# A gated linear attention with a mixture of attention experts on one core: the table that sets the order of the work is drawn anew

## The chip, the cores and the metric

The kernel runs on one core of one Trainium2 chip. The metric is the device time of one execution in microseconds (us). Each of the core's engines takes its own instructions in order and waits on semaphores for the others: PE (TensorE, matrix products and transposes), DVE (VectorE), ACT (ScalarE), POOL (GpSimd) and SP (SyncE, which here only issues DMA transfers). All of this kernel's transfers, loads and stores, are issued from SP.

## The reference, cut to what matters

```
for t in range(768):                                  # 4 batches x 8 heads, D = 48
    state = alpha[t] * state + outer(k[t], v[t])
    y[t] = q[t] @ state
x = heads of y side by side                           # 4 x 768 x 384
top two of four experts per token, by x @ w_gate; w = their softmax
for e in range(4):                                    # causal attention of one head of 64
    a = softmax(mask(x @ wq[e] @ (x @ wk[e]).T / 8))
    out += (w of e, 0 if not chosen) * (a @ (x @ wv[e]) @ wo[e])
```

## The kernel before

**Tiles.** The time axis is cut into 24 chunks of 128 steps, chunk n = 6 * batch + c. Each chunk has three inputs: `al` (the decays, 258.5 KB), `qk` (512 KB) and `vt` (v, 256 KB). Each of the three has four buffers (al_71 to al_74, qk_75 to qk_78, vt_79 to vt_82), so a load waits until the chunk that held its buffer is done with it. A chunk goes through: scan of the decays backwards (DVE L470) with its reciprocal (L474); scan forwards (L493); k times the backward products (L497) and q times the forward products (L501), the two instructions that need `qk`; the 128 x 128 products of q and k (PE L537), masked on DVE (L548) or on ACT and POOL (L552, L556); transposes of k (PE L570, copied on ACT); the state's update (PE L589, DVE L601 or L604, POOL L606, ACT L611), which needs `vt`; the chunk's output (PE L635), which needs `vt` too, and its split into a rounded part xh (ACT L651) and a rest xl (DVE L655). A check of the decays (ACT L513) reads `al` last and sets its buffer free. For the first three chunks the output goes to the buffer x32 instead (ACT L660).

Three chunks make one unit of the expert part, of which there are eight: projections to q and k (PE L683, or the fp32 form at L910 for unit 0, copied out at L691 to L695) and to v and the gate (L702, L710), scores (L772), their row maximum (DVE L782), exponentials (ACT L791), scaling by the chosen expert's weight (DVE L803, L804, POOL L810), transposes (PE L828, copied at L842), the product with v (L865) and with wo (L891), and the store (SP L899). Unit 0 also splits the weights in two parts (DVE L412 to L423).

**The order.** `build` lists all 1574 operations once, each with what it reads and writes. `schedule` walks the table `ORDER`, a permutation of their numbers, and works out a start for each from its own costs of operations and DMAs; from these starts come two things only: which buffer of a kind each tile gets, and how many idle matmuls (`warm`, L1118) stand at the very start of PE's queue where the model has PE wait. `emit` then issues the operations in the order of the table. Each engine works through its part of that list in order, so the table alone decides what stands behind what on PE, DVE, ACT and POOL, and in which order SP issues the transfers: a load that waits for its buffer holds every later load and store on SP.

**Loads.** load_al (L381), load_q (L385), load_v (L390), the weights wqk (L395), wvg and wo (L397, L398). In the trace the n-th transfer is issued only when the (n - 8)-th has landed. The table asks for chunk 5's three inputs twice.

Of the kernel before, what the change touches and what calls it, by code (L numbers as in the profile page):

```python
# [17 lines left out]
B, H, S, D = 4, 8, 768, 48  # L18
# [31 lines left out]
DMA_FIXED = 1.5  # L50
DMA_RATE = 400.0
# [92 lines left out]
def turnover(a, b):  # L144
    a, b = FORM[a], FORM[b]
    return 0.0 if a == b else NEAR.get(a + b, LEAVE[a] + ENTER[b])


class Plan:

# [1079 lines left out]
```

## Time and profile before

| | us |
|---|---|
| three runs | 317.69, 317.56, 316.7; median 317.56 |
| the profiled execution's own time | 316.78 |
| its span in the trace | 315.0 |
| PE busy | 302.0, 96% of the span |
| PE weight loads | 269.6, 86% |
| DVE busy | 246.6, 78% |
| ACT busy | 225.5, 72% |
| POOL busy | 118.7, 38% |

The granted TensorE clock is 1.00 through the whole span. PE is busy nearly everywhere, so what is left besides PE's own work is the stretch at the start in which the first data arrive, some short waits of PE, and the tail behind its last product. The page of the profile says how long each engine was busy; which wait cost something is read from the chain of waits and from each engine's timeline, where a bracket gives the idle time ahead of a group of instructions and what ended it.

### The profile page before, as it was taken

What the parts mean: (1) busy time and instruction counts of PE and PEld (TensorE: products, weight loads), DVE (VectorE), ACT (ScalarE), POOL (GpSimd) and SP (SyncE); (2) the same over time, 40 slices, a digit from 0 to 9 for tenths busy, and PEclk for the clock granted to TensorE, in tenths of its full rate; (3) what the DMA queues carried; (4) which work ended last, traced back from release to release, by engine and by line L of the source; (5) the groups of instructions that cost most, each with busy time, mean ns of one, the idle gap of its engine ahead of it and who ended that gap; (6) DMA issues with size and microseconds to landing.
All of it is one profiled execution on the core that took longest, in us unless ns stands there. A gap on an engine that the chain in (4) does not pass through costs nothing.

```text
span 315.0 us, 9747 instructions
## 1 busy us (share of the span) xinstructions
PE 302.0 (96%) x3786; PEld 269.6 (86%) x3786; DVE 246.6 (78%) x711; ACT 225.5 (72%) x592; POOL 118.7 (38%) x188
## 2 busy tenths in 40 slices
PE   6798999999999999999999999989999999999994
PEld 4697989999899799989988977979989978797883
DVE  6899999998999999997897998559677565658440
ACT  2476777689877796779488894468778797479681
POOL 4053144435256326216425341162454315316240
PEclk9999999999999999999999999999999999999999
DMA  6967363161340236415611530412100010010111
GB/s 208 406 233 238 126 233 140 34 201 62 127 145 25 73 145 207 139 31 195 222 38 36 189 108 0 152 56 74 37 17 2 27 51 2 1 52 25 52 52 57
DMA packets 15027, 33.25 MB, mean 106 GB/s; under 512 B 1664, under 2 KB 4992, under 8 KB 14976
## 3 DMA queue, kind: packets, MB, share of 16 engines
q1 hardware_dynamic: 14976, 32.58, 30.3%
q8 instruction: 31, 0.51, 0.6%
q14 instruction: 20, 0.16, 0.2%
HBM read 27.86 MB, written 4.72 MB: 103 GB/s over the span
## 4 chain that ended last, share of the span: by engine, by line
PE 75%; DVE 10%; DMA 9%; issue 1%; SPq 1%; POOL 1%; ACT 1%; DVEq 0%; POOLq 0%
PE g L683 12%; PE g L828 11%; PE g L865 11%; PE g L772 10%; PE g L635 9%; DMA qk<-in_qk_dram 9%; PE g L891 8%; PE g L537 5%; PE g L710 5%; PE g L589 2%; PE g L570 2%; DVE al L493 2%; DVE a L782 1%; POOL a L810 1%; DVE qk L497 1%
## 5 line engine op out<-in xcount | busy, mean ns | idle before, releaser
L810 POOL TENSOR_SCALAR a<-a,cf,gw 128x256 f32<-128x256 f32 (+5 forms) x96 | 81.9, 863 | 90.4 <-DVE cf L804 60.4
L791 ACT ACTIVATE a<-a,mx 128x128 f32<-128x128 f32 (+5 forms) x96 | 63.4, 663 | 16.5 <-DVE mx L782 16.1
L842 ACT ACTIVATE at<-g 128x512 f32<-128x512 f32 (+3 forms) x124 | 50.3, 462 | 9.5 <-PE g L828 8.8
L782 DVE CUSTOM_DVE_ANT_0 a<-g,cm 128x512 f32<-128x512 f32 (+3 forms) x96 | 48.1, 529 | 8.6 <-PE g L772 7.0
L828 PE MATMUL g<-ident,a 128*128 128x128 f32 x336 | 45.4, 276 | 1.5 <-POOL a L810 0.7
L828 PEld LDWEIGHTS g<-ident,a 128*128 128x128 f32 x336 | 37.6, 141 | 5.9 <-POOL a L810 2.2
L865 PE MATMUL g<-at,vg 128*64 128x384 f32 (+2 forms) x324 | 39.5, 390 | 0.0
L772 PE MATMUL g<-k,q 64*128 64x256 f32 (+3 forms) x384 | 38.4, 334 | 0.0
L865 PEld LDWEIGHTS g<-at,vg 128*64 128x64 f32 x324 | 24.1, 137 | 13.6 <-issue 8.6
L635 PE MATMUL g<-ms,vt 128*32 128x128 f32 x768 | 32.8, 274 | 0.4 <-DVE mx L782 0.4
L772 PEld LDWEIGHTS g<-k,q 64*128 64x128 f32 x384 | 29.9, 185 | 3.7 <-DVE mx L782 0.8
L470 DVE TENSOR_TENSOR_SCAN al<-al,d1r 112x516 f32<-112x516 f32 (+1 forms) x25 | 29.9, 1200 | 3.8 <-DMA al<-in_al_dram 3.8
L556 POOL TENSOR_SCALAR_AFFINE_SELECT ms<-ms 128x512 f32<-128x512 f32 x23 | 14.6, 637 | 47.1 <-ACT ms L552 47.0
L493 DVE TENSOR_TENSOR_SCAN al<-al,d1c 112x516 f32<-112x516 f32 (+1 forms) x25 | 31.7, 1268 | 0.1
L683 PE MATMUL g<-xh,wqk_h 128*128 128x384 f32 x84 | 29.1, 346 | 0.0
L683 PE MATMUL g<-xh,wqk_l 128*128 128x384 f32 x84 | 28.3, 337 | 0.0
L683 PE MATMUL g<-xl,wqk_h 128*128 128x384 f32 x84 | 28.3, 336 | 0.0
L513 ACT ACTIVATE al<-al 112x1033 f32<-112x1033 f32 x24 | 25.5, 1064 | 2.7 <-POOL a L810 1.5
L537 PE MATMUL g<-qk 48*128 48x128 f32 x384 | 25.1, 276 | 0.0
L537 PEld LDWEIGHTS g<-qk 48*128 48x128 f32 x384 | 23.4, 187 | 1.2 <-issue 0.3
L635 PE MATMUL g<-qk,S 112*32 112x128 f32 x480 | 24.2, 272 | 0.0
L606 POOL TENSOR_TENSOR C<-C,ev 112x192 f32<-112x192 f32 x16 | 12.9, 808 | 29.0 <-DVE C L604 21.4
(103 smaller groups left out, 636.4 us busy)
## 6 DMA issues: line engine op xcount, KB each, us to landing
qk<-in_qk_dram SPq DMA_DIRECT2D x24, 512.0 KB, 4.7
vt<-in_v_dram SPq DMA_DIRECT2D x25, 256.0 KB, 3.5
al<-in_al_dram SPq DMA_DIRECT2D x24, 258.5 KB, 2.9
out_dram<-ot SPq DMA_DIRECT2D x24, 192.0 KB, 1.9
at<-in_wqk_dram SPq DMA_DIRECT2D x1, 768.0 KB, 7.9
qk<-in_qk_dram SPq DMA_DIRECT2D x2, 256.0 KB, 4.2
at<-in_wvg_dram SPq DMA_DIRECT2D x1, 390.0 KB, 9.5
at<-in_wo_dram SPq DMA_DIRECT2D x1, 384.0 KB, 9.8
```

The source lines that it names most:

```text
L470: V.tensor_tensor_scan(backwards(al[0:P, AW + c0 - 1:AW + c1 - 1]), backwards(al[0:P, c0:c1]), d1r[0:P, sl].rearrange("p a w -> p (a w)"), ...
L493: V.tensor_tensor_scan(c, c, T(("d1c", n))[0:P, sl].rearrange("p a w -> p (a w)"), 0.0, OP.mult, OP.max)
L537: PE.matmul(T(("pa", n, s))[:, C * p:C * p + C], t[r:r + D, p, C:2 * C], t[r:r + D, p, 0:C], start=True, stop=True, tile_position=(r, 0))
L635: PE.matmul(py[32 * j:32 * j + 32, k], l, r, start=(i == 0), stop=(i == len(parts) - 1), tile_position=(0, 32 * j))
L683: PE.matmul(pj[:, :W3], w[:, kt, cs], x[:, kt, :], start=(i == 0), stop=(i == 8))
L772: PE.matmul(T(sk[e])[:, :w], q[r, x, ts], k[r, y, c0:c1], start=(m == 0), stop=(m == 2), tile_position=(64 * e, 0))
L782: V.tensor_tensor_reduce(T(ak[e])[:, c0:c1], T(sk[e])[:, :w], cm[:, m0:m0 + w], -1.0, mx[:, 0:1] if x else BIG, OP.add, OP.min, accum_out= ...
L791: A.activation(a[:, 0:n], a[:, 0:n], AF.Exp, bias=T(mk)[:, e, len(pieces) - 1:len(pieces)], scale=-1.0, accum_out=T(("sm", u))[:, ix:ix + 1])
L810: G.tensor_scalar(a[:, 0:n], a[:, 0:n], T(ck_)[:, e:e + 1], T(("gw", u))[:, i, eg:eg + 1], op0=OP.mult, op1=OP.mult)
L828: PE.transpose(pt[:, 128 * (j - j0):128 * (j - j0) + 128], a[:, 128 * j:128 * j + 128], ident)
L842: A.activation(dst, src, AF.Copy)
L865: PE.matmul(py[64 * e:64 * e + 64, lo:n1], v[:, j % 3, 64 * eg:64 * eg + 64], at[e][:, at_off(j) + lo:at_off(j) + n1], start=(j == 0), sto ...
```

## The change

The table is another permutation of the same 1574 operations: the same instructions on each engine, in another order. The constants of the model's DMA become slower: 1.7 us and 390 KB/us instead of 1.5 us and 400 KB/us, and 240 KB/us until 8 us after the start (`DMA_EARLY`, in the new function `landing`); the separate rate of the weights is dropped. The table was drawn with these costs, and judged on runs of the model in which DMAs are late by a random amount. The number of idle matmuls at the start goes from 33 (23, 5 and 5) to 43 (32 and 11). Lines of the new kernel stand 1 to 7 further down: L381, L385 and L390 are L388, L392 and L397 there, L497 and L501 are L504 and L508, L655 is L662.

```diff
-DMA_FIXED = 1.5
-DMA_RATE = 400.0
+DMA_FIXED = 1.7
+DMA_RATE = 390.0
+DMA_EARLY = (8.0, 240.0)
...
 ORDER = (
-    13, 4, 14, 6, 0, 2, 7, 8, 1, 3, 10, 21, 31, 22, 60, 23, 9, 32, 24, 26, 25, 34, 28, 33, 15, 30, 35, 61, 16, 27, 36,
...
+    4, 6, 0, 7, 2, 21, 31, 22, 32, 14, 8, 13, 1, 3, 10, 9, 18, 23, 17, 60, 33, 24, 26, 34, 36, 25, 61, 57, 35, 68, 27,
...
+def landing(t, kb, rate):
+    until, early = DMA_EARLY
+    first = min(kb, max(0.0, until - t) * early)
+    return t + first / early + (kb - first) / rate
...
-                dma_at = max(t + DMA_FIXED, dma_at) + o["dma"] / (o["rate"] or DMA_RATE) / 1e3
+                dma_at = landing(max(t + DMA_FIXED, dma_at), o["dma"] / 1e3, o["rate"] or DMA_RATE)
...
-                op("S", 0.43, 0, lambda T: SY.dma_start(wqk(T), wqk_d), w=whole(("at", -2)), dma=786432, rate=360)
+                op("S", 0.43, 0, lambda T: SY.dma_start(wqk(T), wqk_d), w=whole(("at", -2)), dma=786432)
...
-                op("S", 0.43, 0, lambda T: SY.dma_start(wv(T), wv_d), w=[(("at", -1), 0)], dma=399360, rate=360)
-                op("S", 0.43, 0, lambda T: SY.dma_start(wo(T), wo_d), w=[(("at", -1), 1)], dma=393216, rate=360)
+                op("S", 0.43, 0, lambda T: SY.dma_start(wv(T), wv_d), w=[(("at", -1), 0)], dma=399360)
+                op("S", 0.43, 0, lambda T: SY.dma_start(wo(T), wo_d), w=[(("at", -1), 1)], dma=393216)
```

**SP at the start**, behind the loads of chunks 0 and 1 up to qk_76. Before, vt_80 is chunk 1, al_73 and qk_77 are chunk 3, vt_81 is chunk 8, al_74 and qk_78 are chunk 2, and chunk 2's v is two rows below the last one shown:

```order
L390 DMA vt_79<-in_v_dram 128x512
L390 DMA vt_80<-in_v_dram 128x512
L381 DMA al_73<-in_al_dram 128x517
L385 DMA qk_77<-in_qk_dram 128x1024
L395 DMA at_136<-in_wqk_dram 128x1536
L390 DMA vt_81<-in_v_dram 128x512
L381 DMA al_74<-in_al_dram 128x517
L385 DMA qk_78<-in_qk_dram 128x1024
L397 DMA at_138<-in_wvg_dram 128x780
L398 DMA at_138<-in_wo_dram 128x768
L381 DMA al_72<-in_al_dram 128x517
L390 DMA vt_82<-in_v_dram 128x512
```

Now, al_73 and qk_77 are chunk 2, al_74 and qk_78 chunk 3, vt_80 is chunk 1, vt_81 chunk 4 and vt_82 chunk 2:

```order
L397 DMA vt_79<-in_v_dram 128x512
L402 DMA at_136<-in_wqk_dram 128x1536
L388 DMA al_73<-in_al_dram 128x517
L388 DMA al_74<-in_al_dram 128x517
L397 DMA vt_80<-in_v_dram 128x512
L392 DMA qk_77<-in_qk_dram 128x1024
L397 DMA vt_81<-in_v_dram 128x512
L392 DMA qk_78<-in_qk_dram 128x1024
L404 DMA at_138<-in_wvg_dram 128x780
L405 DMA at_138<-in_wo_dram 128x768
L397 DMA vt_82<-in_v_dram 128x512
L388 DMA al_72<-in_al_dram 128x517
```

Chunk 2's qk moves from the fourteenth to the twelfth load and chunk 3's takes the fourteenth place; chunk 2's v moves from the twentieth place to the seventeenth.

**DVE at the start**, from the update of the state of chunk 1. Before, chunk 2 is al_74 with qk_78 and chunk 3 is al_73 with qk_77:

```order
L604 TENSOR_TENSOR C_93<-g_69,C_92 112x192
L474 RECIPROCAL d1c_87<-al_74 112x4
L497 TENSOR_TENSOR qk_78<-qk_78,al_74 112x4x128
L493 SCALAR_TENSOR_TENSOR al_74<-al_74,d1c_87 112x516
L695 TENSOR_TENSOR k_103<-g_67,k_103 128x128
L501 TENSOR_TENSOR qk_78<-qk_78,al_74 112x4x128
```

Now chunk 2 is al_73 with qk_77, and chunk 3 al_74 with qk_78:

```order
L611 TENSOR_TENSOR C_93<-g_63,C_92 112x192
L504 TENSOR_TENSOR qk_77<-qk_77,al_73 112x4x128
L481 RECIPROCAL d1c_87<-al_73 112x4
L504 TENSOR_TENSOR qk_78<-qk_78,al_74 112x4x128
L500 SCALAR_TENSOR_TENSOR al_73<-al_73,d1c_87 112x516
L702 TENSOR_TENSOR k_104<-g_67,k_104 128x128
L508 TENSOR_TENSOR qk_77<-qk_77,al_73 112x4x128
```

The k product of chunk 3 moves up to behind that of chunk 2, ahead of chunk 2's forward scan.

**SP some 198 us into the execution.** Before, vt_82 is chunk 23, qk_75 is chunk 20 and qk_76 chunk 21:

```order
L899 DMA out_dram<-ot_144 128x384
L385 DMA qk_76<-in_qk_dram 128x1024
L381 DMA al_74<-in_al_dram 128x517
L390 DMA vt_82<-in_v_dram 128x512
L385 DMA qk_75<-in_qk_dram 128x1024
L899 DMA out_dram<-ot_145 128x384
```

Now chunk 20 is qk_76 (and chunk 23's qk is qk_77), and chunk 23's v, vt_80 in the last row, stands behind three more loads:

```order
L392 DMA qk_77<-in_qk_dram 128x1024
L392 DMA qk_76<-in_qk_dram 128x1024
L906 DMA out_dram<-ot_145 128x384
L397 DMA vt_79<-in_v_dram 128x512
L388 DMA al_74<-in_al_dram 128x517
L392 DMA qk_78<-in_qk_dram 128x1024
L906 DMA out_dram<-ot_145 128x384
L397 DMA vt_80<-in_v_dram 128x512
```

The load of chunk 20's qk no longer stands behind the load of a v that is wanted three chunks later.

**DVE at the same place**, where the rests xl of two chunks of unit 6 are formed (xl_99). Before, qk_75 is chunk 20:

```order
L497 TENSOR_TENSOR qk_76<-qk_76,al_71 112x4x128
L782 ISA a_135,mx_116<-g_63,cm 128x384
L782 ISA mx_116 128x1
L655 TENSOR_TENSOR xl_99<-g_66,xh_97 128x3x128
L501 TENSOR_TENSOR qk_75<-qk_75,al_73 112x4x128
L782 ISA a_129,mx_119<-g_68,cm 128x128
L782 ISA mx_119 128x1
L655 TENSOR_TENSOR xl_99<-g_69,xh_97 128x3x128
L803 TENSOR_SCALAR cf_122<-sm_114 128x2
```

Now qk_76 is chunk 20:

```order
L662 TENSOR_TENSOR xl_99<-g_68,xh_97 128x3x128
L789 ISA a_128,mx_120<-g_67,cm 128x128
L789 ISA mx_120 128x1
L662 TENSOR_TENSOR xl_99<-g_69,xh_97 128x3x128
L508 TENSOR_TENSOR qk_77<-qk_77,al_71 112x4x128
L810 TENSOR_SCALAR cf_123<-sm_114 128x2
L811 RECIPROCAL cf_123<-cf_123 128x2
L504 TENSOR_TENSOR qk_76<-qk_76,al_72 112x4x128
```

Both rests stand ahead of the first instruction that needs chunk 20's qk; before, one stands behind it.

**At 149 us**, SP's queue held, before, the qk of chunks 19 and 17, the v of 18, the qk of 16, the v of 19, and then the qk of 18. Now it holds the v of 16 and the qk of 16, 18 and 19, then a store, and only then the v of 18 and 19, the decays of 23 and the v of 17. Further up, chunk 5's second load of v (vt_79) now stands behind the decays and the qk of chunk 6 and the v of chunk 6; before, it stood ahead of the first two.

## Rows read from the trace of the kernel before

**Rows 1.** The page: span, and engines by busy time, share and instructions.

```profile
span 315.0 us, 9747 instructions
...
PE 302.0 (96%) x3786; PEld 269.6 (86%) x3786; DVE 246.6 (78%) x711; ACT 225.5 (72%) x592; POOL 118.7 (38%) x188
```

**Rows 2.** Windows: stretch, length, busy time of PE, PEld, DVE, ACT, POOL, clock, DMA share, GB/s.

```profile
0.00:20.00 20.00, 15.14 (x205) 12.31 (x209) 14.97 (x29) 8.12 (x16) 6.89 (x37) 1.00 0.76 278
20.00:40.00 20.00, 19.15 (x299) 17.54 (x288) 19.52 (x50) 14.08 (x40) 4.55 (x8) 1.00 0.61 200
200.00:220.00 20.00, 18.40 (x221) 17.33 (x220) 11.94 (x39) 13.55 (x44) 6.83 (x11) 1.00 0.29 98
```

**Rows 3.** The chain of waits: start, length, what. A DMA runs from issue to landing.

```profile
8.78 9.23 DMA qk<-in_qk_dram
...
150.57 6.65 DMA qk<-in_qk_dram
...
198.08 5.80 DMA qk<-in_qk_dram
```

**Rows 4.** DVE timeline, start: start, length, instruction, count, idle before and what ended it.

```profile
15.28 1.23 DVE L470 TENSOR_TENSOR_SCAN al<-al,d1r 112x516 f32<-112x516 f32 x1 [1.31 <-DMA al<-in_al_dram]
...
18.03 0.69 DVE L497 TENSOR_TENSOR qk<-qk,al 112x512 f32<-112x512 f32 x1 [0.58 <-DMA qk<-in_qk_dram]
...
26.72 0.35 DVE L604 TENSOR_TENSOR C<-g,C 112x192 f32<-112x192 f32 x1
```

**Rows 5.** PE timeline at the start.

```profile
8.24 0.71 PE L1118 MATMUL g<-ot 128*128 128x256 bf16 x5
9.46 0.34 PE L589 MATMUL g<-vt,kt 128*64 128x48 f32 x5 [0.51 <-DMA vt<-in_v_dram]
...
15.95 2.94 PE L910 MATMUL g<-at,at 128*128 128x128 f32 x24 [1.31 <-ACT at L660]
...
25.90 0.64 PE L589 MATMUL g<-vt,kt 128*64 128x48 f32 x16 [0.81 <-ACT k L691]
```

**Rows 6.** SP timeline up to 50 us (SPq: the issues of transfers).

```profile
20.32 0.85 SPq L390 DMA_DIRECT2D vt<-in_v_dram  x2
...
33.00 6.20 SPq L390 DMA_DIRECT2D vt<-in_v_dram  x3
39.26 0.90 SPq L381 DMA_DIRECT2D al<-in_al_dram  x2
...
47.88 0.33 SPq L390 DMA_DIRECT2D vt<-in_v_dram  x1
```

**Rows 7.** SP timeline, 140 to 200 us.

```profile
149.38 1.10 SPq L390 DMA_DIRECT2D vt<-in_v_dram  x1
...
197.70 0.33 SPq L390 DMA_DIRECT2D vt<-in_v_dram  x1
198.08 1.83 SPq L385 DMA_DIRECT2D qk<-in_qk_dram  x1
```

**Rows 8.** DVE timeline at 157 and 203 us.

```profile
157.25 0.69 DVE L497 TENSOR_TENSOR qk<-qk,al 112x512 f32<-112x512 f32 x1 [1.29 <-DMA qk<-in_qk_dram]
...
203.90 0.69 DVE L501 TENSOR_TENSOR qk<-qk,al 112x512 f32<-112x512 f32 x1 [3.31 <-DMA qk<-in_qk_dram]
```

**Rows 9.** PE timeline, five places.

```profile
47.86 0.41 PE L635 MATMUL g<-ms,vt 128*32 128x128 f32 x8
...
83.00 0.42 PE L635 MATMUL g<-ms,vt 128*32 128x128 f32 x8 [0.42 <-DVE mx L782]
...
158.55 0.63 PE L828 MATMUL g<-ident,a 128*128 128x128 f32 x4 [0.42 <-DVE k L695]
...
205.33 0.39 PE L710 MATMUL g<-wv_h,xl 128*128 128x260 f32 x1 [0.86 <-DVE xl L655]
...
208.26 0.33 PE L828 MATMUL g<-ident,a 128*128 128x128 f32 x1 [0.74 <-POOL a L810]
```

**Rows 10.** Tile vt, 19 to 27 us: its transfers, three of them issued there.

```profile
DMA to landing us min/median/max: 3.1/5.4/5.6
```

146 rows, old and new, of the table ORDER are left out of this document.

## The prediction

> **What bounds the kernel now.** The page comes first. PE is busy for 302.0 of 315.0 us [rows 1], and the change neither adds nor removes an instruction of PE except idle matmuls, so the time can move only where PE waits: at the start, in the waits between, and in the tail behind the last product. The reader should then look for where the missing 13 us lie. In the windows the first 20 us hold 15.14 us of PE's work and the next 20 hold 19.15, with DVE at 14.97 and 19.52 [rows 2]: at the start PE waits for data, and from 20 to 40 us DVE is as full as PE. From 200 to 220 us PE has 18.40, with DVE only 11.94 busy: a hole without a full engine beside it. The chain of waits says what makes these holes. It goes back through transfers of `qk` at three places, one issued at 8.78 us and 9.23 us on its way, one at 150.57 with 6.65, one at 198.08 with 5.80 [rows 3]. The timelines of DVE and PE say what each of them costs, and SP's why the transfer was late. So the sum has three gains, one for each place, and one loss, for waits that the new order makes.
>
> **The start.** DVE waits 1.31 us until 15.28 for the decays of chunk 2 and 0.58 us until 18.03 for its qk, the fourteenth load [rows 4]. Behind that it runs nearly without a gap up to the state's update at 26.72, and it stays almost full until 40 us; a lead of DVE is therefore a lead of what follows. In the new order the fourteenth load is chunk 3's qk, with the same bytes ahead of it (four al, four qk, three vt and wqk, 4.73 MB), so I take the same landing, 18.0. The wait of 1.31 us goes, since both scans' decays are now the ninth and tenth loads, but DVE then only waits the longer for the fourteenth. It does so at the same place of its queue, but it has by then done the k product of chunk 2, whose qk is now the twelfth load and comes before DVE is at it. That instruction takes 0.69 us alone and its neighbours begin 0.61 behind it [rows 4], so DVE is about 0.65 us ahead from there: **-0.65**. PE had a wait of 0.81 us at 25.90, which the row puts down to ACT [rows 5]; ACT had been done, and the later releaser is chunk 2's v: the issues at 20.32 [rows 6] with a median of 5.4 us to landing [rows 10] give 25.7. That v is now the seventeenth load instead of the twentieth and is issued when the ninth lands, some 8 us earlier; the wait goes, but what follows on PE waits for DVE, so 0.81 is not added to 0.65. The low end is both waits of this stretch gone, 0.58 + 0.81 = 1.4; the other end is half the lead, 0.3, if PE meets DVE again further on.
>
> Of the ten more idle matmuls four lie in one run at the very start, while nothing has arrived. Eleven now stand a little further down, where five took 0.71 us [rows 5]; eleven would take 1.6, or 0.9 more. Half of that lies in PE's wait of 0.51 us for chunk 0's v right behind it [rows 5]; the other 0.4 us I cost at nothing, since DVE's lead sets the pace further on, and keep as an upper bound.
>
> What the start would be by a page: the Trainium skill ("DMA: Bandwidth & Descriptors", section "Specifications") gives some 358 GB/s from HBM for one core. By it, as an estimate, the 4.73 MB would be in 13.2 us after the first issue, some 3 us before DVE wants them in the new order. The trace disagrees: the window from 0 to 20 us moved 278 GB/s [rows 2], and the fourteenth load took until 18.0.
>
> **At 157 us.** DVE waited 1.29 us for the qk of chunk 18 [rows 8], and PE 0.42 us for DVE's next instruction [rows 9]; with the pause ahead of that group about 0.6 us was lost. The load was issued at 150.57, behind the v of chunk 19, whose issue took 1.10 us [rows 7], and behind the qk of 16 issued just before that; it took 6.65 us because three loads of 0.25 to 0.5 MB were on the way with it. In the new order the qk of 18 stands ahead of the v of 18 and 19. From the end of the work that frees its buffer to its first use PE has 6 to 8 us of work, and a qk by itself takes some 4 us to land, as the one at 198.08 shows (5.80, less the 1.83 of its issue, is 4.0) [rows 3, 7]: a margin of about 2 us. **-0.6**; the bounds are 0 (as late as before) and -0.6.
>
> **At 204 us.** This is the largest term. The v of chunk 23, needed 40 us of work later, waited for its buffer and went out at 197.70; the qk of chunk 20 behind it went out at 198.08 and took 1.83 us to issue [rows 7] and 5.80 to land [rows 3]. DVE sat idle 3.31 us [rows 8], with the rest xl of chunk 19 queued behind the waiting instruction. PE waited 0.86 us for that rest, then 0.74 for POOL, which had itself waited for the reciprocals behind it on DVE [rows 9]; with the idle pieces between the groups, the distance between PE's clock and its own work grew by 2.0 us over these places. In the new order both rests and the reciprocals of one tile stand ahead of the first instruction that needs this qk, and the load stands ahead of the v of chunk 23. PE has 6.7 us of work between the end of chunk 18, which frees the buffer, and the first use; the load needs 4.0 by the same row, or 5.8 if it is as slow as the row. **-2.0**; the other end is half of it, if DVE waits for the qk all the same with PE's next input behind it (0.86 [rows 9]) and POOL after that.
>
> **New waits.** PE has single waits of 0.3 to 0.4 us with no transfer in them, like the one at 83.00 behind a row maximum (0.42 [rows 9]); three of them, about 1.0 us together. Walking both orders with the trace's durations, the places where PE's input is ready less than 0.4 us ahead are about ten before and fifteen now. Half as many again of 1.0 is **+0.5**; bounds 0 and +2.1 (each of the five new ones as dear as the 0.42).
>
> The tail behind the last product holds the same work: 0.
>
> **The sum.** 316.78 (the profiled execution; its span is 315.0, and 1.78 lies around it) - 0.65 - 0.6 - 2.0 + 0.5 = 314.0. The profiled execution stands 0.78 below the median of the three runs shown, near the lowest of them; of that I add half to the sum, since a median is asked for: **314.4 us**.
>
> **The rivals.**
> - *No change.* The gains are eaten: DVE, full until 40 us and more, gives the lead at the start back, and the place at 204 us is only half mended while the new short waits cost their upper bound. 316.78 - 0.3 - 0.3 - 1.0 + 1.5 = 316.7, with the same 0.4 for the median 317.1. For it speaks that three unlike places must all work; against it that the rows of 204 us name one cause, a load behind another, and the new order takes that apart.
> - *Slower, by chunk 5's v.* Its second load now stands behind the decays of chunk 6, which wait for the check of chunk 4, and behind the qk and the v of chunk 6. PE needs it for the output of chunk 5, at 47.86 before [rows 9], and so at about 47.2. From 39.26, when the decays of chunk 6 went out, four loads of 1.58 MB held SP's queue until 47.88 [rows 6]; by that rate, 250 KB/us with 2.2 us for the first, 1.31 MB are in at about 45.9. The margin is 1.3 us; each further microsecond is one of PE, since every later product of PE stands behind this one. It decides when the check ends more than 1.3 us later than before, and it makes the kernel slower when that is over 4.5 us: about 318.9 us. For it speaks that ACT has copies of the projections there; against it that PE's work in front of the check is the same.
> - *The fourteenth load comes early:* chunk 3's qk lands before DVE is at it, and the wait of 0.58 us [rows 4] goes with the lead of 0.65: 314.4 - 0.6 = 313.8. Against it speaks that the same bytes stand ahead of that load as before; for it only that rate of the Trainium skill.
> - *The change does not do what it says:* the loads' order does not move what ends the waits, since the transfers are as late as the bytes ahead make them, and the order only changes which chunk is late. Then the start and 157 us give nothing, 204 us gives half, and the idle matmuls cost 0.4: 316.78 - 1.0 + 0.4 + 0.5 = 316.7, again 317.1 for the median.
>
> **How the numbers follow.** The forecast gets 0.58, the early fourteenth load 0.05, no change 0.15, the change without effect 0.08, slower 0.14. A measurement of this kernel tells a difference from 0.3%, 0.95 us: faster is below 316.6 and slower above 318.5. Of the forecast's own cases a small part comes out above 316.6 by its bounds, and of the two cases at 317.1 a third comes out below it. So faster 0.70, the same 0.17, slower 0.13. The forecast's own bounds are 311.9 (start -1.4, no new waits, the profile's own time taken as the median: 316.78 - 1.4 - 0.6 - 2.0 = 312.8, and 0.9 more if the short waits of today go too) and 316.4 (start -0.3, nothing at 157, half of the place at 204, and the 0.4 for the median). The range goes on to the two cases at 317.1 and stops short of the slower one: 311.9 to 318.0.
>
> **What would show it.** In the profile after: PE's window from 200 to 220 us above 19.5; no wait of DVE over 1 us for qk at 157 or 204 us; chunk 2's v landing before 21 us and no wait of PE at its first use; DVE's k product of chunk 3 starting at about 18.0, with that of chunk 2 done before. It is wrong if PE waits over 1 us at the output of chunk 5, near 47 us, if the fourteenth load comes much later than 18, or if short waits for DVE, ACT and POOL add up to more than 2.5 us.

## The result, and the profile after

The changed kernel takes **314.31 us** (median of 4 runs, 314.15 to 314.53) against 317.13 for the kernel before beside it (4 runs, 316.66 to 317.69): a ratio of **0.9911 [0.9889, 0.9933]**, 2.8 us less, where 314.4 was forecast. The profiled execution took 314.38.

The page, its span and its first part (they answer to [rows 1]):

```profile
span 312.6 us, 9798 instructions
...
PE 302.4 (97%) x3796; PEld 270.7 (87%) x3796; DVE 244.9 (78%) x711; ACT 226.6 (72%) x592; POOL 118.3 (38%) x188
```

The span is 2.4 us shorter, and PE's busy time is 0.4 longer by the ten idle matmuls: PE lost 13.0 us before and 10.2 now. Windows, with the columns of [rows 2]:

```profile
0.00:20.00 20.00, 16.59 (x223) 13.81 (x227) 16.22 (x31) 8.24 (x16) 7.39 (x38) 1.00 0.89 313
20.00:40.00 20.00, 20.00 (x313) 18.31 (x301) 18.54 (x48) 14.35 (x41) 3.51 (x7) 1.00 0.53 171
...
200.00:220.00 20.00, 20.00 (x234) 19.26 (x233) 15.67 (x45) 14.78 (x46) 8.34 (x12) 1.00 0.24 73
220.00:240.00 20.00, 19.15 (x256) 17.23 (x259) 15.33 (x48) 15.97 (x39) 7.99 (x12) 1.00 0.06 22
```

The hole from 200 to 220 us is closed (18.40 before), and PE is full from 20 to 40 us (19.15 before). A new hole of 0.85 us has opened from 220 to 240 us, where PE had 19.99 before. Only reading on shows that the total hides losses as well as gains.

**The start.** DVE's timeline; where nothing stands in brackets, the engine did not wait:

```profile
16.66 0.68 DVE L504 TENSOR_TENSOR qk<-qk,al 112x512 f32<-112x512 f32 x1
...
17.34 0.66 DVE L504 TENSOR_TENSOR qk<-qk,al 112x512 f32<-112x512 f32 x1
...
25.37 0.36 DVE L611 TENSOR_TENSOR C<-g,C 112x192 f32<-112x192 f32 x1
```

PE at the same place, and SP's issue of chunk 2's v (20.32 before, [rows 6]):

```profile
24.59 0.67 PE L596 MATMUL g<-vt,kt 128*64 128x48 f32 x16
```

```profile
12.58 0.33 SPq L397 DMA_DIRECT2D vt<-in_v_dram  x1
```

The k products of chunks 2 and 3 follow one another with no wait; both waits of [rows 4] are gone. Chunk 2's v landed at 20.65, and PE's wait of 0.81 us [rows 5] with it.

**At 157 and 204 us.** DVE, then SP:

```profile
155.56 1.29 DVE L504 TENSOR_TENSOR qk<-qk,al 112x512 f32<-112x512 f32 x2 [2.81 <-DMA qk<-in_qk_dram]
156.77 0.55 DVE L702 TENSOR_TENSOR k<-g,k 128x384 fp32r<-128x384 f32 x1
...
199.44 0.56 DVE L662 TENSOR_TENSOR xl<-g,xh 128x384 fp32r<-128x384 f32 x1
...
201.06 0.67 DVE L504 TENSOR_TENSOR qk<-qk,al 112x512 f32<-112x512 f32 x1
```

```profile
193.97 0.33 SPq L392 DMA_DIRECT2D qk<-in_qk_dram  x1
...
208.18 0.42 SPq L397 DMA_DIRECT2D vt<-in_v_dram  x1
```

At 204 us the load of chunk 20's qk goes out 4.1 us earlier, lands at 197.85, and DVE uses it at 201.06 with no wait, where [rows 8] had 3.31; the v of chunk 23 goes out at 208.18. At 157 us DVE waits longer than before, 2.81 us against 1.29, now for chunk 19's qk (landed 155.54); but only one k product stands behind it, and PE does not wait.

**New waits.** PE:

```profile
42.62 0.89 PE L779 MATMUL g<-k,q 64*128 64x384 f32 x6 [0.45 <-DVE C L611]
...
99.02 2.21 PE L835 MATMUL g<-ident,a 128*128 128x128 f32 x17 [0.99 <-DVE gw L752]
...
232.91 1.31 PE L835 MATMUL g<-ident,a 128*128 128x128 f32 x10 [0.85 <-DVE xl L662]
```

These are the waits that the experiments call those at 41, 97 and 231 us. What DVE did ahead of the last of them, and what POOL did meanwhile (L739 to L744 are unit 6's router, the gate):

```profile
229.38 0.33 DVE L739 TENSOR_TENSOR gw<-vg,gm 128x12 f32<-128x12 f32 x1
...
229.76 0.76 DVE L741 TENSOR_TENSOR gt<-vg 128x48 f32<-128x48 f32 x1
230.44 1.47 DVE L742 TENSOR_TENSOR gt<-gt,lm 128x48 f32<-128x48 f32 x1
231.95 0.21 DVE L743 TENSOR_TENSOR gt<-gt 128x48 f32<-128x48 f32 x1
...
232.31 0.55 DVE L662 TENSOR_TENSOR xl<-g,xh 128x384 fp32r<-128x384 f32 x1
```

```profile
229.66 0.54 POOL L613 TENSOR_TENSOR C<-C,ev 112x192 f32<-112x192 f32 x1
230.19 1.67 POOL L817 TENSOR_SCALAR a<-a,cf,gw 128x512 f32<-128x512 f32 x2
```

L742 takes 0.20 us at most other places of this trace; here it takes 1.47, and it ends at 231.91, when POOL's two scalings end (231.86). The rest xl, for which PE's transposes wait by the row above, stands right behind the gate.

**Where the time went, place by place.** At each of the points below PE has done the same products in both traces, but for the ten idle matmuls, so the start of one same output product can be compared directly (after minus before, us):

| up to | difference | step |
|---|---|---|
| output of chunk 2 | -1.34 | start -1.34 |
| chunk 6 (67 us) | -0.44 | +0.90: the wait at 42 us and smaller ones |
| chunk 8 (82 us) | -1.02 | -0.58: the wait of 0.42 at 83 us [rows 9] is gone |
| chunk 10 (116 us) | +0.19 | +1.21: the wait at 99 us |
| chunk 15 (149 us) | +0.20 | 0 |
| chunk 18 | -0.34 | -0.54: the place at 157 us |
| chunk 20 (214 us) | -2.38 | -2.04: the place at 204 us |
| chunk 22 (239 us) | -1.55 | +0.83: the wait at 232 us |
| last output | -2.12 | -0.57, nearly all of it between 257 and 270 us: not traced to a cause |
| span | -2.4 | -0.27: the last stores landed 2.28 us after their issue, 2.60 before |

### The profile page after: what moved, and what is told of

The parts are those of the page before. It is cut to its first block, busy times and chain, and to the rows that moved or that the text cites. A ratio compares the mean times of both kernels' runs of the same rounds, so it can differ in the third digit from the quotient of the medians.

```text
span 312.6 us, 9798 instructions
## 1 busy us (share of the span) xinstructions
PE 302.4 (97%) x3796; PEld 270.7 (87%) x3796; DVE 244.9 (78%) x711; ACT 226.6 (72%) x592; POOL 118.3 (38%) x188
## 5 line engine op out<-in xcount | busy, mean ns | idle before, releaser
L817 POOL TENSOR_SCALAR a<-a,cf,gw 128x512 f32<-128x512 f32 (+5 forms) x96 | 81.6, 860 | 96.7 <-DVE cf L811 54.1
L798 ACT ACTIVATE a<-a,mx 128x256 f32<-128x256 f32 (+5 forms) x96 | 63.4, 662 | 11.6 <-DVE mx L789 11.1
L789 DVE CUSTOM_DVE_ANT_0 a<-g,cm 128x384 f32<-128x384 f32 (+3 forms) x96 | 47.8, 528 | 6.7 <-PE g L779 5.6
L779 PE MATMUL g<-k,q 64*128 64x256 f32 (+3 forms) x384 | 37.7, 332 | 0.5 <-DVE C L611 0.5
L477 DVE TENSOR_TENSOR_SCAN al<-al,d1r 112x516 f32<-112x516 f32 (+1 forms) x25 | 30.9, 1245 | 1.7 <-DMA al<-in_al_dram 1.7
L642 PEld LDWEIGHTS g<-ms,vt 128*32 128x32 f32 x768 | 21.0, 109 | 2.3 <-issue 0.6
```

The costliest lines, as they stand in the source:

```text
L477: V.tensor_tensor_scan(backwards(al[0:P, AW + c0 - 1:AW + c1 - 1]), backwards(al[0:P, c0:c1]), d1r[0:P, sl].rearrange("p a w -> p (a w)"), ...
L642: PE.matmul(py[32 * j:32 * j + 32, k], l, r, start=(i == 0), stop=(i == len(parts) - 1), tile_position=(0, 32 * j))
L779: PE.matmul(T(sk[e])[:, :w], q[r, x, ts], k[r, y, c0:c1], start=(m == 0), stop=(m == 2), tile_position=(64 * e, 0))
L789: V.tensor_tensor_reduce(T(ak[e])[:, c0:c1], T(sk[e])[:, :w], cm[:, m0:m0 + w], -1.0, mx[:, 0:1] if x else BIG, OP.add, OP.min, accum_out= ...
L798: A.activation(a[:, 0:n], a[:, 0:n], AF.Exp, bias=T(mk)[:, e, len(pieces) - 1:len(pieces)], scale=-1.0, accum_out=T(("sm", u))[:, ix:ix + 1])
L817: G.tensor_scalar(a[:, 0:n], a[:, 0:n], T(ck_)[:, e:e + 1], T(("gw", u))[:, i, eg:eg + 1], op0=OP.mult, op1=OP.mult)
```

## The experiments

Each gain of a place below is taken against the first trace of the kernel before; the ratios compare all runs of a variant with the runs of the kernel before beside them. The theory: two loads account for the gain, chunk 20's qk (204 us) and chunk 2's v (start), each held behind a transfer of no urgency; and the new order gives part of it back where the gate's instructions on DVE are stretched by POOL with a PSUM-freeing rest behind them. The rival: the gain lies in the constants and idle matmuls, or is spread over many places, and the named loads give nothing alone. All edits move single operations of the table (numbers are its operations).

### One load alone: b_q20

```
 pl.schedule(ORDER)
+for x, y in ((981, 1155),):        # chunk 20's qk ahead of chunk 23's v
+    pl.order.remove(x); pl.order.insert(pl.order.index(y), x)
```

> The table of before with one transfer moved: the qk of chunk 20 goes ahead of the v of chunk 23 on SP, everything else as before. Theory (a late load in front of queued work): the qk's buffer is free when the products of chunk 18 end (194.2 us), the v's only at 197.7, so the load goes out 3 us earlier, at about 194.5, lands near 199, DVE's wait of 3.31 us at 203.9 is gone and PE gains the whole 2.0 us of that place: about 315.1 against 317.1. Rival (the place is lost by the order of DVE and POOL there, and the load only marks it): PE gains under 0.5 us, 316.7 or more.

Measured: 314.78 (12 runs), ratio 0.9964 [0.9938, 0.9989]. SP and then PE of its trace:

```profile
193.96 0.33 SPq L385 DMA_DIRECT2D qk<-in_qk_dram  x1
197.41 0.33 SPq L390 DMA_DIRECT2D vt<-in_v_dram  x1
```

```profile
26.14 0.64 PE L589 MATMUL g<-vt,kt 128*64 128x48 f32 x16 [1.55 <-DMA vt<-in_v_dram]
```

The place at 204 us gains 2.11 us by one moved load; its window holds 20.00 us of PE. The ratio is only 1.1 us less than the runs of before beside it: their median was near 315.9 and not 317.1, and some of them lose less at this place (before3 below). The load leaves at 193.96, when chunk 18's products of q and k (PE L537) have read the buffer, not at the end of chunk 18. The second row is as telling: here qk landed early (16.03), DVE was ahead, and PE waited all the longer for chunk 2's v. At 157 us this execution of the old order lost nothing.

### The loads as late, the queue behind them cleared: b_k

```
-L501 TENSOR_TENSOR qk_75<-qk_75,al_73 112x4x128
 L782 ISA a_129,mx_119<-g_68,cm 128x128
 ...
 L804 RECIPROCAL cf_126<-cf_126 128x2
+L501 TENSOR_TENSOR qk_75<-qk_75,al_73 112x4x128
```

and, at 157 us, the k product that waits for chunk 18's qk moved behind the rest of the projections' k (L695).

> The table of before with all transfers left as late as they were; only two instructions of DVE move, each behind work that was queued behind it: the k product of chunk 18 goes behind the rest of the projections' k (157 us), the q product of chunk 20 goes to just ahead of its k product, behind the rest xl of chunk 18 and three pairs of reciprocals (204 us). Theory (the wait costs PE only through what is queued behind the waiting instruction): DVE still waits for both loads, about 1 us and 3 us, but PE gains 0.5 at 157 and 2.0 at 204 us: 314.6. Rival (PE needs the late qk itself, for the transposes of chunks 18 and 20 that follow): the waits of PE move to those transposes, and less than 1.0 in all is gained: 316.1 or more.

Measured: 314.26 (12 runs), 0.9968 [0.9944, 0.9991]. DVE:

```profile
199.63 0.55 DVE L655 TENSOR_TENSOR xl<-g,xh 128x384 fp32r<-128x384 f32 x1
...
201.95 0.17 DVE L804 RECIPROCAL cf<-cf 128x2 f32<-128x2 f32 x1
202.72 1.09 DVE L501 TENSOR_TENSOR qk<-qk,al 112x512 f32<-112x512 f32 x1 [0.60 <-DMA qk<-in_qk_dram]
```

The load landed at 202.70, nearly as late as before (203.88), since PE was 1.1 us further ahead here; the rest and the reciprocals were done, DVE had 0.60 us left to wait, and PE none. The place gained 2.10, as much as with the early load; against the runs beside it the variant takes 1.0 us less. A late load costs what is queued behind the instruction that waits for it.

### The constants without the table: b_const

The new planner constants with the old table; of the schedule only the idle matmuls differ (29 and 7 for 23, 5 and 5).

```
-DMA_FIXED = 1.5
-DMA_RATE = 400.0
+DMA_FIXED = 1.7
+DMA_RATE = 390.0
+DMA_EARLY = (8.0, 240.0)
```

> The new constants and the new landing rule with the table of before. The order and all buffers are those of before; only the idle matmuls at the start become 29 and 7 instead of 23, 5 and 5. Theory: the constants act only through the table that was drawn with them, so 317.1 within 0.6. Rival (the idle matmuls at the start are part of what the change brings): over 0.6 us faster or slower.

Measured: 315.74 (10 runs), 0.9991 [0.9968, 1.0013]: no change against the runs beside it, though the 317.1 itself was missed. The rival falls.

### Chunk 2's v alone: b_v2

The load of chunk 2's v (operation 20) takes the place of operation 303 in the table, and the other way round.

```
-... 75, 101, 303, 66, ...    -... 44, 80, 20, 51, ...
+... 75, 101, 20, 66, ...     +... 44, 80, 303, 51, ...
```

> The table of before with two loads exchanged: the v of chunk 2 takes the twelfth place of the v of chunk 8, and that the twentieth; nothing else at the start moves. Theory (the late v of chunk 2, 25.8 us, is what bounds the start: it holds PE at the state's update of chunk 2, and in runs whose fourteenth load came a microsecond earlier PE only waited the longer for it): the wait of 0.8 to 1.7 us at 25 us is gone and PE is 0.7 to 1.3 us ahead at the output of chunk 2. Rival (the prediction's: DVE sets the pace there, with the fourteenth load): PE is less than 0.3 us ahead at that output.

Measured: 315.06 (11 runs), 0.9954 [0.9927, 0.9981]. Its profiled execution is its slowest, 318.49. PE:

```profile
8.09 0.39 PE L570 MATMUL g<-ident,qk 112*128 112x112 f32 x2 [2.15 <-DVE qk L497]
...
27.85 0.67 PE L589 MATMUL g<-vt,kt 128*64 128x48 f32 x16
```

The wait for the v is gone and 0.96 us is gained from the output of chunk 1 to that of chunk 2. Before that, this execution lost more: PE stood idle for 2.15 us, and the granted clock then was 0.50 until about 15 us. The median shows the gain, this trace its mechanism; the 318.49 is not what the edit costs.

### All of it in the old table: b_all

The swap of b_v2, and after the table:

```
+for x, y in ((845, 986), (981, 1155)):   # b_k's k product at 157 us, b_q20's load
```

> The table of before with four operations moved: the v of chunk 2 and that of chunk 8 exchanged, the qk of chunk 20 ahead of the v of chunk 23, the k product of chunk 18 behind a rest at 157 us. Theory (these three places are all that the new table gains): as fast as the new table or up to 1 us faster, since the three new waits of that one are not there: 313.3 to 314.4. Rival (the gains of the places don't add up, because DVE is full up to 180 us and takes the lead of the start back): 314.8 or more, as with the load of chunk 20 alone.

Measured: 313.72 (8 runs), 0.9905 [0.9872, 0.9939]; -0.74 between the outputs of chunks 1 and 2, -0.65 at 157 us, -2.11 at 204. Four operations moved by hand reach the new table, in which 1492 of the 1574 places hold another operation. The -0.65 at 157 us is not the edit's: before2 and before3 below have it without any. The ratios of b_q20 and b_v2 multiply to 0.992, so within the noise the two loads are the whole gain.

### Does the after kernel repeat? after2

> The changed kernel once more, beside before on the same chip, since before's runs spread from 314.2 to 317.4 us in the last job. Theory (what the new table takes away is the part of before's loss that depends on when transfers land): after's runs spread less than before's, all within 1.2 us, with the median near 314.3, and the three new waits of PE (41, 97 and 231 us) stand in its trace again, since they come from the order on DVE and POOL and not from transfers. Rival: after's runs spread like before's, and the new waits are those of one run.

Measured: 314.44 (7 runs, 313.69 to 314.91), 0.9935 [0.9908, 0.9963]. The waits at 41, 97 and 231 us (0.25, 1.16 and 1.01) are there again, and the gain at 204 us (-2.05): they belong to the order. The output of chunk 2 is 1.36 us ahead again, but by another way: 0.92 of it stands already at the output of chunk 1 (0.08 in the first trace of after), and DVE waits 0.94 us for the fourteenth load.

### And the kernel before? before2, before3

> The kernel before once more, for a second look at its trace, since its runs fall into two groups, 314.2 to 315.9 and 316.3 to 317.5 us. Theory (the groups are the place at 204 us, where PE loses either nothing or 2.0 us, as chunk 20's qk lands before or after PE wants the rest behind it): if the run is one of the lower group, PE loses under 0.5 us there and the transfer lands before 202.5; if it is one of the upper group, PE loses 1.6 to 2.0 there as in the first trace. Rival (the groups come from the start, where PE waits for the first data and its clock may fall): the loss at 204 us is 1.6 to 2.0 in either group, and a run of the lower group shows 1.5 us less before 35 us.

> The kernel before for a third look at its trace: the first two (316.8 and 317.2 us) are of the upper group of its runs. Theory (the lower group, 314.2 to 315.9, are runs in which PE loses nothing at 204 us): a run of the lower group loses under 0.5 us there, because the load of chunk 20's qk is issued faster than in 1.8 us or lands before 202.5; one of the upper group loses 1.6 to 2.2 there again. Rival (the lower group gains its 2 us elsewhere): a run of the lower group loses 1.6 to 2.2 there all the same.

The kernel before unchanged: 317.16 and 314.77. SP of the first and of the second, then DVE and PE of the second:

```profile
197.84 1.84 SPq L385 DMA_DIRECT2D qk<-in_qk_dram  x1
```

```profile
197.09 0.42 SPq L385 DMA_DIRECT2D qk<-in_qk_dram  x1
```

```profile
201.74 0.70 DVE L501 TENSOR_TENSOR qk<-qk,al 112x512 f32<-112x512 f32 x1 [2.13 <-DMA qk<-in_qk_dram]
...
206.10 0.33 PE L828 MATMUL g<-ident,a 128*128 128x128 f32 x1 [0.69 <-POOL a L810]
```

The issue of one load took 1.84 us in one execution and 0.42 in the other; the place at 204 us lost 2.15 and 0.84. That is 1.3 of the 2.4 us between the two times. Against the first trace (316.78) before3 lost 1.2 us less at 204, 0.66 less at 157 and 0.33 less at 82 us. I had expected under 0.5 to be lost at 204 in the shorter one: the mechanism held, the size did not. Neither of them lost anything at 157 us.

### POOL's hold on the gate: a_pool

Four of POOL's scalings of unit 5, three of which run beside or just ahead of the gate of unit 6, work on 8 columns instead of 512 or 640; the kernel leaves the other columns unscaled.

```
-G.tensor_scalar(a[:, 0:n], a[:, 0:n], ...
+m = 8 if (u, pair) == (5, 0) and i < 2 else n
+G.tensor_scalar(a[:, 0:m], a[:, 0:m], ...
```

> The new table, with POOL's scaling of two tiles of unit 5 (pair 0, the first two) cut to 8 of their columns; the rest of these scores stays unscaled. Theory (an instruction of DVE's gate is held until POOL's running instruction ends): the seven instructions of the gate of unit 6 at 230 us take 1.1 to 1.4 us instead of 3.3, none over 0.4, and the wait of PE at 231.5 (1.02) falls below 0.3. Rival (these instructions are long for another reason): they stay near 0.8 and 1.5 us and PE's wait stays.

Measured: 313.26, one run. DVE:

```profile
228.89 0.20 DVE L741 TENSOR_TENSOR gt<-vg 128x48 f32<-128x48 f32 x1
229.01 0.20 DVE L742 TENSOR_TENSOR gt<-gt,lm 128x48 f32<-128x48 f32 x1
```

These two instructions are not stretched any more, and PE's wait at 231 us is gone. That POOL's scalings stretch the gate is shown; that PE waited for what stands behind the gate, and not for POOL's shorter work itself, is shown by a_fix below, where the scalings stay whole.

### Moving the rests ahead of the gate: a_two, a_fix, a_fix2

a_two moves one rest ahead of the gate, at 97 and at 231 us (the second piece is shown); a_fix adds the reciprocals at 97 us, moves the whole gate of unit 6 back, and moves what frees C at 41; a_fix2 leaves 41 us alone and takes the second rest at 97 along.

```
+L662 TENSOR_TENSOR xl_98<-g_69,xh_96 128x3x128
 L738 TENSOR_REDUCE gm_110<-vg_108 128x3
 ...
 L744 TENSOR_REDUCE gt_109<-gt_109 128x12
-L662 TENSOR_TENSOR xl_98<-g_69,xh_96 128x3x128
 L611 TENSOR_TENSOR C_92<-g_68,C_93 112x192
```

> The new table with three operations moved, at the two places where its trace shows new waits of PE (1.16 us at 97.4 and 1.02 at 231.5): the rest k of a projection (and its copy on ACT) goes ahead of the gate of unit 2 on DVE, and the rest xl of chunk 21 ahead of the gate of unit 6. Theory (DVE's gate is stretched by POOL's scaling, and PE waits for what stands behind the gate): the gates stay as long as they are (1.8 and 3.3 us instead of 1.1), PE loses nothing there, and the kernel takes 0.9 + 0.8 less: 312.6 against 314.3. Rival (PE waits there for POOL's scaled scores, and the DVE instruction only ended about then): the waits stay, 314.0 or more.

> The new table with operations moved at the three places of its new waits; transfers and buffers stay. At 97 us the reciprocals of the third tile and its exponentials go ahead of the rests of two projections, so that POOL starts 1.3 us earlier, and the gate of unit 2 goes behind one more rest; at 231 us the gate of unit 6 goes 13 us back, to where DVE and POOL are idle; at 41 us one rest q goes ahead of the gate of unit 0 and a rest k ahead of the state's update. Theory (PE waits for whatever stands behind the stretched gate on DVE, or behind POOL, which starts late for the same reason): 1.0 + 0.9 + 0.3 less than the new table, about 312.2. Rival (the next thing is as late, as at 97 us when only one rest was moved): under 0.7 less.

> The new table with operations moved at two places: at 97 us the third tile's exponentials and reciprocals go ahead of two rests of projections, and both rests that stood behind the gate of unit 2, or behind its second part, go ahead of it; at 231 us the gate of unit 6 goes 13 us back. The order at 41 us is that of the new table, since moving it changed nothing. Theory (PE waits at 97 us for one rest after another behind the gate, as the last version still did 4 us later): no wait over 0.4 us from 90 to 104 us and none at 231, 1.9 us less than the new table, about 312.5. Rival (the lead is given back within 20 us because DVE is full there): under 1.0 less, 313.5 or more.

Measured: a_two 314.59 (12 runs), 0.9966 [0.9944, 0.9988]: a miss. PE of a_two:

```profile
98.13 1.31 PE L835 MATMUL g<-ident,a 128*128 128x128 f32 x10 [0.45 <-POOL a L817]
100.30 1.31 PE L835 MATMUL g<-ident,a 128*128 128x128 f32 x10 [0.85 <-DVE q L702]
...
232.75 0.84 PE L835 MATMUL g<-ident,a 128*128 128x128 f32 x6 [0.55 <-DVE C L611]
```

One wait became two at 97 us, and at 231 us the state's update behind the gate took the rest's place, with L739 stretched to 1.94 us. a_fix: 313.78 (5 runs), 0.9907 [0.9878, 0.9937]. With the gate moved away from POOL's scalings, which stay as they are, the wait at 231 us is gone; 41 us is unchanged, and at 99 to 101 us the next rest, behind the gate's second part, costs 1.08. a_fix2: **313.41** (6 runs, 313.13 to 313.67), **0.9891 [0.9848, 0.9934]**, the shortest of those that do the whole work, under both kernels. Its window and its PE at 99 us:

```profile
220.00:240.00 20.00, 20.00 (x305) 18.32 (x308) 13.57 (x47) 16.02 (x39) 8.52 (x13) 1.00 0.06 22
```

```profile
99.06 2.58 PE L835 MATMUL g<-ident,a 128*128 128x128 f32 x20 [0.62 <-ACT at L849]
```

The window is full again. At 97 us 0.78 of 1.16 us stays: with both rests early, PE next meets ACT's copy. It gained 0.9 on the median of the after kernel, where 312.5 us had been expected.

## Why the prediction was right, and where not

**204 us: right, -2.04 for -2.0.** Both halves of the cause were shown apart: the load early (b_q20, -2.11) or the queue behind the waiting instruction cleared (b_k, -2.10). One detail was wrong: the buffer comes free with chunk 18's products of q and k, so the margin was larger than I allowed: 7.1 us from issue to use, not 6.7. And the size is that of one kind of execution: with an issue of 0.42 us instead of 1.8, the order of before loses 0.84 (before3), and in the medians the moved load gave 1.1 us.

**The start: -1.34 for -0.65, within its low bound of 1.4.** The step that failed is "the wait goes, but what follows on PE waits for DVE, so 0.81 is not added to 0.65". PE at 25 us waited for chunk 2's v, not for DVE: where DVE was early, the wait for the v only grew (b_q20, 1.55 us), and where the v alone was early, 0.96 us came (b_v2). The landing of the fourteenth load was the other miss: 17.16 for 18.0, so the condition of the rival of the early load came true in this trace. In six executions of the old load order it came between 16.03 and 18.01: one trace had given me its late end.

How large the lead is still depends on the loads. The new order was the same up to this point in six executions (after, after2 and four variants with edits further on), and the output of chunk 2 was 0.62 to 2.03 us ahead of the first trace of before. The two smallest leads, 0.62 and 0.84 (a_fix and a_fix2), go with the latest landings of the fourteenth load, 18.49 and 18.28. There DVE waited 1.6 us for it, much as the prediction had it, and PE 0.5 us for an ACT copy behind ACT's own wait for the weights wo (1.1 us); in a_fix2:

```profile
18.37 0.69 DVE L504 TENSOR_TENSOR qk<-qk,al 112x512 f32<-112x512 f32 x1 [1.63 <-DMA qk<-in_qk_dram]
...
21.85 1.60 PE L917 MATMUL g<-at,at 128*128 128x128 f32 x12 [0.54 <-ACT at L667]
```

Five executions of the old order (before, before2, before3, b_q20, b_k) lie within 0.5 us of each other there, with landings 2.0 us apart: in them chunk 2's v held PE whatever came earlier. That the late loads make the small leads is read from these traces; no edit moved those loads alone. So -1.34 is one draw, in the middle of its range.

The 278 GB/s of the first 20 us, by which I called the loads slow, is a mean with nearly empty ends: the trace of before moved 7 GB/s until 2 us and 28 from 18 us on, but 406 from 8 to 16 us.

**157 us: about -0.5 for -0.6, by another way, and a gain on one trace only.** DVE's wait was to go below 1 us; it is 2.81. What changed is what stands behind it. Of the kernel before and its variants only the first trace lost 0.6 here; before2, before3, b_q20 and b_const lost nothing.

**New waits: about +1.8 net for +0.5, within the bound of 2.1.** By the table: 0.90 + 1.21 + 0.83, less 0.58 at 82 us and 0.57 late in the span. The three waits alone, 0.62, 1.16 and 1.02 from start to start of PE's instructions (0.17 more each than the brackets show), pass the 2.5 us that I had named as a sign of error. The term that failed is this one: it counted tight places and took each as a short wait, at most 0.42 us; it missed that one DVE instruction can become seven times as long. That is shown for the third wait. At the second L742 takes 0.83 us, 0.63 more than its 0.20, which is not enough for 1.16. At the first nothing is stretched: the gate's instructions take 0.13 to 0.21 us each there, and the state's update, for which PE waits, stands behind them. In the third, L742 ends as POOL's scalings end, and a_pool sets it back to 0.20. The Trainium skill ("SBUF — State Buffer", section "Who interferes with whom") says that a DVE instruction with two inputs in SBUF and a GpSimd instruction that reads SBUF block each other for a whole instruction, the one that comes first winning. The trace agrees, and is harsher: L742 began at 230.44, during the first of the two scalings of 0.83 us, and did not get in between them. But not every overlap holds: in a_pool L741 and L742 took 0.20 us each while a scaling of 8 columns ran from 228.80 to 229.27. In the kernel before the same gate was stretched less (0.55 and 0.60 us for its second and third instruction, 0.20 for this one), and PE did not wait behind it. The planner's costs hold no such stall.

**Tail 0: about right** (-0.27, which is no gain of the order: in after2 the tail is 0.38 longer than in the first trace of before). **Chunk 5's v:** the rival did not come; its second load landed at 44.05 and PE did not wait for it near 47 us. **The 0.4 for the median: not borne out.** The terms alone gave 314.0, and the profiled execution of after took 314.38: misses of -0.7 at the start, +1.3 for new waits and -0.3 in the tail made that difference, not a median above the profile. Nor was 317.2 a good middle of before. Nearly all of its runs lie from 314.2 to 317.7; the profiled one and the four of the first comparison all lie in the upper part. Beside 14 other runs of before the same kernel after gave 0.9935, some 2.1 us less. The 11 runs of after lie from 313.7 to 314.9, closer together than those of before.

So the places are right and the total fits partly by luck: a start that gave 0.7 us more and a tail that gave 0.3 more nearly cancel new waits that cost 1.3 more. Open remain the -0.57 late in the span, which all six executions of the new order have (0.5 to 0.6 between 257 and 270 us), the -0.58 at 82 us, what makes an issue on SP take 0.4 or 1.8 us, the wait at 41 us, and most of the wait at 97 us, which three rearrangements only moved.

## What to carry to other kernels

Price a late load by what is queued behind the instruction that waits for it, and look first for a load whose buffer is free but which stands behind one whose buffer is not: one moved load gave 2.1 us here against one execution, and 1.1 us in the medians. Take several executions of the kernel before pricing a wait, since two of the places here were dear in one execution and cheap in the next. Ask of a wait what would hold the engine next once it is gone. An order made safe against late transfers can lose to what it does not model: keep what another engine waits for out from behind a run of DVE instructions that POOL can hold.

## What the runs showed of the hardware

Beside POOL's scalings of 512 columns or more, short DVE instructions with two SBUF operands ended within 0.05 us of one of POOL's: L742's 0.20 us became 1.47 and 0.83, L739's 0.17 became 1.94 (a_two). Beside scalings of 8 columns L741 and L742 kept their 0.20 us (a_pool).

In each of the 14 traces one DMA issue on SP that starts between 196.9 and 199.6 us takes 1.28 to 1.84 us, where most issues take 0.33 to 0.44, whichever transfer stands there (a qk, a store; the decays at 197.78 for 1.45 us in the after kernel).

The granted clock fell to 0.50, TensorE's level of 1.2 GHz, in two executions at the start: after 2.15 us of idle PE in b_v2, for about 7 us, and after 1.81 us in b_const, from about 16 to 19 us. After 1.31 us in the kernel before [rows 5] it stayed at 1.00. The window in b_const (columns of [rows 2]):

```profile
16.00:18.50 2.50, 2.50 (x12) 2.50 (x13) 2.50 (x6) 0.32 (x1) 2.04 (x11) 0.50 0.61 241
```

Its 24 matmuls of L917 took 4.52 us there, where [rows 5] has 2.94 for the same: a wait for ACT of half a microsecond more cost 1.6 us beyond itself.
